# Causal masks of five batches moved from VectorE to GpSimd, and half a batch's loads reshaped, in an attention and mixer kernel

## The chip, the cores and the metric

The kernel runs on one core of one Trainium2 chip. A core has TensorE (matmul; the profile shows its matmuls as PE and its weight loads as PEld), VectorE (DVE), ScalarE (ACT), GpSimd (POOL) and SyncE (SP, which here only issues DMAs). The metric is the device time of one execution in microseconds (us), the median of several runs.

## The reference

Causal attention with a bias from a running sum, then a low rank mix along the sequence and a two layer feed forward block along the channels:

```python
B, H, S, D = 8, 8, 576, 64
scores = q @ k.T / sqrt(D)
cum = cumsum(max(s, 0), axis=-1)
scores = where(causal, -1e9, scores + minimum(-(cum[:, None] - cum[None, :]), 0))
attn = softmax(scores)                       # per batch and head
x = (attn @ v) as [B, S, H * D]              # 8 x 576 x 512
u = x + ((x.T @ U) @ V).T                    # U 576x32, V 32x576
out = u + maximum(u @ w_ch1, 0) @ w_ch2      # 512 -> 2048 -> 512
```

Inputs and output are float32; the kernel computes in bf16 with float32 accumulation.

## The kernel before

**Work units.** The 64 heads are taken in 32 pairs, n = 0 to 31, four pairs to a batch (`PB = 4`, so batch b has n = 4b to 4b + 3). Each pair passes through three generators, whose `yield`s are the points at which other work may be put between:

- `transposes(n)` (T): q and k of the pair, loaded with the sequence on 72 partitions, are turned by TensorE (L314) into PSUM and copied by VectorE or ACT into one of the `slot` tiles (L334 or L337). Rows of the running sum come into the same slot by a DMA on SP's queue (L298), so that the bias is part of the score matmul.
- `scores(n)` (S): score matmuls, transposed, keys on partitions (L401); ACT takes the exponential into a tile `pT` in four instructions, two of 128x1024 for the near blocks of the two heads (L416), one for the middle (L427), one of 128x128 for the tail (L433). The causal masks follow: the four diagonal blocks of each head (128x512) and the tail blocks of both heads (128x128), three masks for a pair.
- `values(n)` (V): matmuls of `pT` with v (L461); VectorE takes a reciprocal of the row sums (L470) and scales (L471) into `x_sb`. From batch 2 on, `x_sb` is also transposed by a DMA on SP (L478) into `xT`.

When a batch is done, `seqmix(b)` makes u transposed, `uT`, from it (VectorE: L499, L505, L515). The rows of u are then taken in nine groups of 512 by `chanmix(g)`: hidden layer matmuls (L647), ReLU on ACT (L807), then the second layer by seven products on quarters (L692) with sums on VectorE before (L674) and after (L706), and a store. `u_sd`, u with the sequence on partitions again, comes from a DMA transpose on SP (L814). In group 1 VectorE also makes sums of the weights (L256).

**Order.** TensorE and GpSimd run in program order (`in_program_order`). Up to n = 9 the order is a written list of steps (`weave`). From n = 8 a loop goes over n and does in each turn `transposes(n + 1)`, `scores(n)`, `values(n - 1)`; between their steps `step_fill` puts in steps of the waiting `chanmix`. At the first pair of a batch `load(b + 1)` comes ahead of that and `load_v(b + 1)` at the end; `seqmix(b - 1)` is spread over the second pair. For VectorE, ACT and SP the program order is fixed in the first part only; later a scheduler sets it, so an edit can move an instruction on SP's queue.

**Masks.** `mask(dst, n_tiles, w, on_pool=False)` (L342) either takes the minimum with a stored tile `keep` on VectorE (L346) or calls `causal` (L148), an `affine_select` on GpSimd (L149) that needs no second input. Batch 0 uses GpSimd through `masks(pT, True)`; for n = 4 to 31 `scores` calls `mask` without the last argument, so VectorE does it.

**Loads.** `load_qk(b, h, n)` (L108) issues the loads of q and k from GpSimd. Without runs (L116) a partition gets eight neighbouring tokens of a head (2 KB of source in one piece); the copies out of PSUM then write with a step, and take the tokens apart (L337). With runs (`in_runs`, b > 2, L111) partition p gets tokens p, p + 72, and so on, in pieces of 64 numbers; the copies then write with unit step (L334). `load(2)` is issued in two halves of four heads, later batches in one piece. `copies` (L288) picks ACT or VectorE. `pT` has two buffers, q and k have two each, slots rotate over three from n = 8 on, and v over two from batch 3 on.

Of the kernel before, what the change touches and what calls it, by code (L numbers as in the profile page):

```python
# [39 lines left out]
def kernel(  # L40
# [24 lines left out]
    PB = NP // B  # L65
# [12 lines left out]
    def pscore():  # L78
        return ps_s.tile([128, 1024], FP32, tag="s", name="pscore")

    def pwork():
        return ps_w.tile([128, 512], FP32, tag="w", name="pwork")
# [19 lines left out]
        q_t[b] = loads.tile([TP, H, TT * D], BF16, tag="q_sd", name="q_sd")  # L102
        k_t[b] = loads.tile([TP, H, TT * D], BF16, tag="k_sd", name="k_sd")

    def in_runs(b):
        return b > 2

    def load_qk(b, h, n):  # L108
        for dst, src in ((q_t[b], q), (k_t[b], k)):
            if in_runs(b):  # L110
                nc.gpsimd.dma_start(  # L111
                    out=dst[:, ds(h, n), :].rearrange("p h (t d) -> p (h t) d", t=TT),
                    in_=src[b, ds(h, n)].rearrange("h (t p) d -> p (h t) d", p=TP),
                )
            else:
                nc.gpsimd.dma_start(  # L116
                    out=dst[:, ds(h, n), :],
                    in_=src[b, ds(h, n)].rearrange("h (p t) d -> p h (t d)", p=TP),
                )
# [6 lines left out]

    alloc_qk(0)
    load_qk(0, 0, 2)
    identity = consts.tile([128, 128], BF16)
    make_identity(nc, identity)  # L130
    load_qk(0, 2, 2)
    load_qk(0, 4, 2)
    load_qk(0, 6, 2)

# [13 lines left out]
    def causal(out, n, w):  # L148
        nc.gpsimd.affine_select(  # L149
            out=out,  # L150
            in_=out,
            compare_op=ALU.is_ge,
            fill=0.0,
            base=0,
            pattern=[[0, n], [1, w]],
            channel_multiplier=-1,
        )
# [45 lines left out]
    def slot_of(n):  # L203
        return slots[n % NSLOT if n < 2 * PB else (n + 1) % 3]
# [8 lines left out]
    def spin(n, dst):  # L213
        for _ in range(n):
            nc.tensor.matmul(
                dst, lhsT=busy[:, 0:128], rhs=busy[:, 0 : dst.shape[1]], start=True, stop=True
            )
# [70 lines left out]
    def copies(n, hh, par):  # L288
        b = n // PB
        on_act = hh == (n == 4) and ((n in (0, 1, 4, 8, 9) or n > 8 and n % PB == 2) or n == 2 and par == 0)  # L290
        return nc.scalar.copy if on_act else nc.vector.tensor_copy

    def transposes(n):
        b, hp = divmod(n, PB)
        slot = slot_of(n)
        if b > 0:
            for r, n_r, c in ((0, 3, 1), (3, 1, 0)):
                nc.sync.dma_start(  # L298
                    out=slot[ds(D + r, n_r), :, ds(c * S, S)],
                    in_=rows_hbm[ds(r, n_r), ds(2 * n, 2)],  # L300
                )
        tps = {}

        def turn(hh, c):
            if c == 0:
                tile = pwork()
                if (n, hh) == (3, 0):
                    spin(2, tile)
                tps[hh] = tile.bitcast(BF16)[:, : 2 * 4 * TP].rearrange(
                    "p (c t m) -> p c t m", c=2, t=4  # L310
                )
            src = (q_t[b], k_t[b])[c]
            for t2 in range(4):
                nc.tensor.transpose(  # L314
                    tps[hh][:, c, t2, :],
                    src[:, 2 * hp + hh, ds(t2 * 128, 128)],
                    identity[:TP, :TP],
                )

        if b == 0:  # L320
            for hh in range(2):
                turn(hh, 0)
            yield
        for hh in range(2):
            if b > 0:
                turn(hh, 0)
            turn(hh, 1)
            tp = tps[hh]
            dst = slot[0:D, hh, 0 : 2 * S]
            for par in range(2):  # L330
                src = tp[par * D : par * D + D]
                if in_runs(b):
                    by_run = dst.rearrange("p (c t two m) -> p c t two m", c=2, t=4, two=2)
                    copies(n, hh, par)(by_run[:, :, :, par, :], src)  # L334
                else:
                    in_turn = dst.rearrange("p (c m t two) -> p c m t two", c=2, t=4, two=2)
                    copies(n, hh, par)(  # L337
                        in_turn[:, :, :, :, par], src.rearrange("p c t m -> p c m t")
                    )
            yield  # L340

    def mask(dst, n_tiles, w, on_pool=False):  # L342
        if on_pool:
            causal(dst, n_tiles, w)
        else:
            nc.vector.tensor_tensor(  # L346
                dst, dst, keep[:, :, 0:w].to_broadcast([128, n_tiles, w]), op=ALU.min
            )
# [48 lines left out]
    def scores(n, pT, spins=()):  # L397
        slot = slot_of(n)

        def mm(dst, hh, j, lo, hi):  # L400
            nc.tensor.matmul(  # L401
                dst,
                lhsT=slot[0:KA, hh, ds(S + j * 128, 128)],
                rhs=slot[0:KA, hh, lo:hi],
                start=True,
                stop=True,
            )

        tail = None
        for hh in range(2) if n > 0 else ():  # L410
            near = pscore()
            for j in range(4):
                mm(near[:, ds(j * 128, 128)], hh, j, j * 128, j * 128 + 128)
            mm(near[:, 512:960], hh, 0, 128, S)
            mm(near[:, 960:1024], hh, 3, 512, S)
            nc.scalar.activation(pT[:, hh, 0:1024], near, EXP, scale=scale)  # L416
            if n >= PB:
                mask(pT[:, hh, 0:512].rearrange("p (a b) -> p a b", a=4), 4, 128)
            if spins:
                tail = tail or pwork()  # L420
                spin(spins[hh], tail)
            yield
        mid, tail = pscore(), tail or pwork()
        for hh in range(2):
            mm(mid[:, ds(hh * 512, 320)], hh, 1, 256, S)
            mm(mid[:, ds(hh * 512 + 320, 192)], hh, 2, 384, S)
        nc.scalar.activation(  # L427
            pT[:, :, 1024:1536], mid.rearrange("p (a b) -> p a b", a=2), EXP, scale=scale
        )
        yield  # L430
        for hh in range(2):
            mm(tail[:, ds(hh * 64, 64)], hh, 4, 512, S)
        nc.scalar.activation(  # L433
            pT[:, :, 1536:1600],
            tail[:, 0:128].rearrange("p (a b) -> p a b", a=2),
            EXP,
            scale=scale,
        )
        if n >= PB:
            mask(pT[:, :, 1536:1600], 2, 64)  # L440
        yield


# [444 lines left out]

    act, dve = nc.scalar.copy, nc.vector.tensor_copy
    S0, S1, S2, S3 = (scores(n, pT_of(n), {1: (2, 3), 3: (2, 0)}.get(n, ())) for n in range(PB))  # L890
    T0, T1, T2, T3 = (transposes(n) for n in range(PB))
    M0, M1, M2, M3 = (mix_first(dt, act) for dt in range(PB))
    A, B_ = (near_by_rows(hh, pT_of(0)) for hh in range(2))
# [82 lines left out]
    def weave(order):  # L976
        for word in order.split():
            if word == "F":
                fill_with(1)
                continue  # L980
            kind, n = word[0], int(word[1:])
            if word not in made:
                if kind == "T":
                    made[word] = transposes(n)
                elif kind == "S":
                    made[word] = scores(n, pT_of(n))
                elif kind == "V":
                    made[word] = values(n, pT_of(n))
                else:
                    made[word] = seqmix(n)  # L990
            step(made[word])
            step_fill()
# [15 lines left out]
    for n in range(2 * PB, NP + 2):  # L1008
        b, hp = divmod(n, PB)
# [62 lines left out]
```

The softmax here doesn't subtract the row's maximum and nothing guards it: scores larger than these inputs give would overflow.

## Time and profile before

| What | Value |
|---|---|
| median of 10 runs (lowest, highest) | 367.28 us (367.01, 367.47) |
| profiled execution | 368.38 us |
| its span, first to last instruction | 366.6 us |
| busy PE, DVE, ACT, POOL | 353.3, 261.8, 204.5, 83.3 us |
| GpSimd's DMA queue q0 | 104,640 packets, 18.49 MB |
| SP's DMA queue q1 | 42,680 packets, 18.11 MB |
| a mask on DVE, 128x512 / on POOL, 128x512 (medians) | 416 ns / 650 ns |
| a copy L337 on DVE / L334 on DVE (medians) | 804 ns / 454 ns |
| granted TensorE clock | 1.00 |

Busy times are unions of an engine's instructions; a busy TensorE is not TensorE at its peak, since its ends are modelled. The chain of waits follows the last instruction back to what released it, step by step. A line number names the line of the kernel that made an instruction. Times inside the span count from its start. Waiting costs time only where the waiting engine is the one that sets the end.

### The profile page before, as it was taken

What the parts mean: (1) busy time and instruction counts of PE and PEld (TensorE: products, weight loads), DVE (VectorE), ACT (ScalarE), POOL (GpSimd) and SP (SyncE); (2) the same over time, 40 slices, a digit from 0 to 9 for tenths busy, and PEclk for the clock granted to TensorE, in tenths of its full rate; (3) what the DMA queues carried; (4) which work ended last, traced back from release to release, by engine and by line L of the source; (5) the groups of instructions that cost most, each with busy time, mean ns of one, the idle gap of its engine ahead of it and who ended that gap; (6) DMA issues with size and microseconds to landing.
All of it is one profiled execution on the core that took longest, in us unless ns stands there. A gap on an engine that the chain in (4) does not pass through costs nothing.

```text
span 366.6 us, 9382 instructions
## 1 busy us (share of the span) xinstructions
PE 353.3 (96%) x3915; PEld 248.5 (68%) x3959; DVE 261.8 (71%) x575; ACT 204.5 (56%) x309; POOL 83.3 (23%) x108
## 2 busy tenths in 40 slices
PE   8998999999999999999999999999999999999995
PEld 3675566665588667876689667876697568477484
DVE  8874776779798758995699559974897178075075
ACT  3873985756663578347843686357734630631720
POOL 8997434404030403140214022000000000000000
PEclk9999999999999999999999999999999999999999
DMA  7999999999949899979994999461014202403202
GB/s 102 175 197 203 169 196 109 158 148 99 105 39 96 145 134 70 100 87 132 128 98 63 143 134 84 58 157 21 18 48 118 64 18 84 91 5 109 61 29 88
DMA packets 147650, 37.40 MB, mean 102 GB/s; under 512 B 130648, under 2 KB 145976, under 8 KB 147608
## 3 DMA queue, kind: packets, MB, share of 16 engines
q0 software_dynamic: 104640, 18.49, 77.6%
q1 hardware_dynamic: 42680, 18.11, 26.4%
q8 instruction: 31, 0.51, 0.6%
q10 hardware_dynamic: 288, 0.20, 0.2%
q14 instruction: 11, 0.09, 0.1%
HBM read 37.25 MB, written 9.70 MB: 128 GB/s over the span
## 4 chain that ended last, share of the span: by engine, by line
PE 76%; DVE 14%; ACT 5%; issue 3%; DMA 1%; DVEq 0%; ACTq 0%
PE pwork L647 28%; PE pwork L692 21%; PE pscore L401 9%; PE pwork L461 7%; PE pwork L314 3%; PE pwork L657 3%; DVE slot L337 3%; ACT hT L807 2%; DVE uT L515 2%; DVE o_sb L706 2%; ACT pT L416 2%; DVE slot L674 2%; PE pscore L363 1%; PE pscore L647 1%; DVE pT L346 1%
## 5 line engine op out<-in xcount | busy, mean ns | idle before, releaser
L647 PE MATMUL pwork<-uT,w_sb 128*128 128x512 bf16 x525 | 133.6, 379 | 3.1 <-DVE x_sb L471 0.8
L807 ACT ACTIVATE hT<-pwork 128x512 bf16<-128x512 f32 x140 | 84.3, 606 | 62.3 <-PE pwork L647 62.2
L416 ACT ACTIVATE pT<-pscore 128x1024 bf16<-128x1024 f32 x56 | 57.2, 1030 | 55.0 <-PE pscore L401 54.1
L647 PEld LDWEIGHTS <-w_sb 128*128 128x128 bf16 x576 | 50.8, 98 | 50.9 <-issue 1.2
L401 PE MATMUL pscore<-slot 68*128 68x320 bf16 (+1 forms) x500 | 56.0, 246 | 0.2
L401 PEld LDWEIGHTS <-slot 68*128 68x128 bf16 x564 | 41.3, 97 | 16.7 <-issue 1.3
L692 PEld LDWEIGHTS <-hT 128*128 128x128 bf16 x496 | 46.2, 98 | 7.5 <-issue 0.7
L185 POOL DMA_DIRECT2D v_slot<-in_v_dram x36 | 30.3, 856 | 81.9 <-PE pwork L461 75.6
L692 PE MATMUL pwork<-w_sb,hT 128*128 128x256 bf16 x384 | 47.5, 273 | 0.0
L346 DVE TENSOR_TENSOR pT<-pT,keep 128x512 bf16<-128x512 bf16 (+1 forms) x81 | 28.6, 353 | 20.8 <-ACT pT L416 14.9
L461 PEld LDWEIGHTS <-pT 128*128 128x128 bf16 x870 | 32.4, 98 | 5.3 <-issue 0.6
L461 PE MATMUL pwork<-v_slot,pT 128*128 128x65 bf16 x870 | 35.5, 193 | 0.2 <-DVE uT L515 0.2
L334 DVE COPY slot<-pwork 64x576 bf16<-64x576 bf16 x70 | 31.6, 452 | 4.5 <-PE pwork L314 3.9
L692 PE MATMUL pwork<-w_sum,slot 128*128 128x256 bf16 x256 | 31.5, 272 | 0.8 <-DVE o_sb L706 0.7
L471 DVE TENSOR_TENSOR x_sb<-pwork,rec 128x320 bf16<-128x320 f32 x64 | 31.1, 488 | 1.3
L337 DVE COPY slot<-pwork 64x576 bf16<-64x576 bf16 x35 | 28.1, 802 | 5.5 <-PE pwork L314 3.5
L427 ACT ACTIVATE pT<-pscore 128x1024 bf16<-128x1024 f32 x29 | 30.2, 1042 | 2.6 <-PE pscore L401 2.4
L674 DVE TENSOR_TENSOR slot<-hT 128x1024 bf16<-128x1024 bf16 x16 | 11.0, 687 | 24.5 <-ACT hT L807 24.3
L470 DVE RECIPROCAL rec<-pwork 128x5 f32<-128x5 f32 x64 | 11.9, 189 | 22.9 <-PE pwork L461 22.7
L692 PEld LDWEIGHTS <-slot 128*128 128x128 bf16 x256 | 24.1, 98 | 4.5 <-issue 1.6
L706 DVE TENSOR_TENSOR o_sb<-o_sb,pwork 128x512 f32<-128x512 f32 (+2 forms) x34 | 21.9, 648 | 1.0 <-PE pwork L692 0.3
L111 POOL DMA_DIRECT2D q_sd<-in_q_dram x5 | 11.2, 2239 | 48.7 <-PE pwork L314 46.3
(128 smaller groups left out, 413.8 us busy)
## 6 DMA issues: line engine op xcount, KB each, us to landing
out_dram<-o_sb SPq DMA_DIRECT2D x35, 256.0 KB
w_sb<-in_moe_w_ch_dram POOLq DMA_DIRECT2D x4, 1024.0 KB, 12.7
v_slot<-in_v_dram POOLq DMA_DIRECT2D x28, 128.0 KB, 6.5
q_sd<-in_q_dram POOLq DMA_DIRECT2D x5, 576.0 KB, 12.1
k_sd<-in_k_dram POOLq DMA_DIRECT2D x5, 576.0 KB, 18.1
q_sd<-in_q_dram POOLq DMA_DIRECT2D x4, 288.0 KB, 12.5
k_sd<-in_k_dram POOLq DMA_DIRECT2D x4, 288.0 KB, 12.2
q_sd<-in_q_dram POOLq DMA_DIRECT2D x4, 144.0 KB, 4.9
```

The lines of the kernel that those rows point to most:

```text
L185: nc.gpsimd.dma_start(out=vt[:rows_t, t, :, 0:D], in_=v[b, :, ds(t * 128, rows_t), :].rearrange("h p d -> p h d"),)
L334: copies(n, hh, par)(by_run[:, :, :, par, :], src)
L337: copies(n, hh, par)(in_turn[:, :, :, :, par], src.rearrange("p c t m -> p c m t"))
L346: nc.vector.tensor_tensor(dst, dst, keep[:, :, 0:w].to_broadcast([128, n_tiles, w]), op=ALU.min)
L401: nc.tensor.matmul(dst, lhsT=slot[0:KA, hh, ds(S + j * 128, 128)], rhs=slot[0:KA, hh, lo:hi], start=True, stop=True,)
L416: nc.scalar.activation(pT[:, hh, 0:1024], near, EXP, scale=scale)
L427: nc.scalar.activation(pT[:, :, 1024:1536], mid.rearrange("p (a b) -> p a b", a=2), EXP, scale=scale)
L461: nc.tensor.matmul(po[:, i, :], lhsT=pT[:, hh, ds(place(j, i), 128)], rhs=vt[:, j, h, :], start=(j == 0), stop=(j == i), skip_group_check= ...
L471: nc.vector.tensor_tensor(x_sb[:, hp, :, ds(hh * D, D)], po[:, :, 0:D], rec.to_broadcast([128, 5, D]), op=ALU.mult,)
L647: nc.tensor.matmul(f1, lhsT=w1_sb[:, kt, ds(nf * 128, 128)], rhs=u[:, kt, :], start=(kt == 0), stop=(kt == 3),)
L692: nc.tensor.matmul(acc[:, i, :], lhsT=a[:, kt, ds(i * 128, 128)], rhs=b[:, kt, :], start=(i == 0 and kt == 0), stop=(kt == HF - 1), skip_g ...
L807: nc.scalar.activation(hT[:, nf, :], f1, RELU)
```

## The change

Two edits. The masks of n = 12 to 31 (batches 3 to 7) are made on GpSimd by `affine_select`; those of n = 4 to 11 stay on VectorE. And the second half (heads 4 to 7) of batch 2's q and k is loaded in runs, so that the copies of n = 10 and 11 have unit step. No other function changes.

```diff
-    def in_runs(b):
-        return b > 2
+    def in_runs(b, h):
+        return b > 2 or b == 2 and h >= 4
 
     def load_qk(b, h, n):
         for dst, src in ((q_t[b], q), (k_t[b], k)):
-            if in_runs(b):
+            if in_runs(b, h):
                 nc.gpsimd.dma_start(
...
                 src = tp[par * D : par * D + D]
-                if in_runs(b):
+                if in_runs(b, 2 * hp):
                     by_run = dst.rearrange("p (c t two m) -> p c t two m", c=2, t=4, two=2)
...
             if n >= PB:
-                mask(pT[:, hh, 0:512].rearrange("p (a b) -> p a b", a=4), 4, 128)
+                mask(pT[:, hh, 0:512].rearrange("p (a b) -> p a b", a=4), 4, 128, n >= 3 * PB)
...
         if n >= PB:
-            mask(pT[:, :, 1536:1600], 2, 64)
+            mask(pT[:, :, 1536:1600], 2, 64, n >= 3 * PB)
```

On GpSimd's queue, in program order, three `affine_select` now stand at each pair from n = 12 on, between the loads that were alone there. On SP's queue the scheduler puts the rows of n = 25 (one of their two DMAs) behind a u_sd transpose, two stores and an xT transpose instead of ahead of them. The orders of TensorE and ACT are the same, apart from the copies of n = 10 having the other form.

## The prediction

> **What bounds the kernel now.** I read the page's table of busy times first, then what TensorE waited for, then busy time by stage, and last the chain of waits inside two short stretches.
>
> ```profile
> PE 353.3 (96%) x3915; PEld 248.5 (68%) x3959; DVE 261.8 (71%) x575; ACT 204.5 (56%) x309; POOL 83.3 (23%) x108
> ```
>
> TensorE is the bound: it is idle for 13.3 us of 366.6. By stage (columns: window, its length, then busy PE, PEld, DVE, ACT, POOL with counts):
>
> ```profile
> 78.00:100.00 22.00, 20.91 (x249) 13.11 (x250) 18.51 (x40) 15.06 (x24) 4.45 (x2) 1.00 2.17 118
> 100.00:292.00 192.00, 189.15 (x2258) 139.73 (x2281) 146.82 (x347) 112.33 (x172) 30.30 (x26) 1.00 0.93 92
> 292.00:360.00 68.00, 67.66 (x503) 46.32 (x506) 38.17 (x64) 24.44 (x41) 0.00 (x0) 1.00 0.21 54
> ```
>
> The change acts from 36 us on and its masks from 102 to 282 us. There TensorE is idle 1.1 us (78 to 100) and 2.9 us (100 to 292), part of it records that the trace lacks. So no relief of another engine can bring more than about 4 us, plus what modelled ends hide. What TensorE waited for, over the whole span:
>
> ```profile
> PE pwork L647 <- DVE x_sb L471: 0.8, 2, 0.6
> PE pwork L692 <- DVE o_sb L706: 0.7, 2, 0.4
> PE pwork L647 <- ACT hT L807: 0.7, 2, 0.5
> PE pwork L461 <- DVE uT L515: 0.2, 1, 0.2
> ```
>
> The first, second and fourth row are VectorE being late. Where it is late, the chain of waits shows what stands in front. First near 86 us (batch 2's last copies, then masks), then near 188 us:
>
> ```profile
> 85.84 0.80 DVE slot L337
> 86.66 0.80 DVE slot L337
> 87.46 0.57 DVE w_sum L256
> 88.03 0.33 DVE pT L346
> ...
> 90.94 0.47 DVE x_sb L471
> ```
>
> ```profile
> 188.13 0.22 DVE pT L346
> 188.35 1.86 DVE uT L515 x4
> 190.21 0.61 DVE o_sb L706
> ```
>
> Both things that the change takes off VectorE (strided copies L337, masks L346) stand on a chain that stops TensorE, but each stop is only 0.2 to 0.6 us as shown. A 72 column matmul is shown with 195 ns although four of them take 0.29 us, so one issues each 32 ns or so, and a shown idle time hides about 0.16 us more.
>
> **What the skill says.** The Trainium skill, "GPSIMD Engine Reference", section on performance versus the Vector engine, says that GpSimd does elementwise work at about half of VectorE's speed. The trace agrees in direction: a mask of 128x512 takes 650 ns on POOL (L149) and 416 on DVE (L346), a factor of 1.6. "SBUF — State Buffer", section "Who interferes with whom", says that a VectorE instruction with two SBUF inputs contends with a GpSimd instruction that reads SBUF, one of the two blocking until the other ends, and that one with at most one SBUF input does not, outside of 2-port modes. Half is seen here: all VectorE copies L337 (PSUM input) lie within 783 to 819 ns, those beside POOL's batch 0 masks included. No L149 overlaps a two input DVE instruction before, so the blocking is not shown. "DMA: Bandwidth & Descriptors", section on why small descriptors are slow, says that short packets carry a fixed overhead each. The trace agrees: 36 to 58 us, with many kilobyte packets, moved 177 GB/s, 58 to 78 us, nearly all under 512 B, 133 GB/s.
>
> **Part 1, batch 2's second half in runs.** Pairs n = 10 and 11 have eight copies. Two (n = 10, first head) run on ACT, six on DVE. DVE: 6 x (804 - 454) ns = 2.1 us saved. ACT: 2 x (799 - 634) = 0.3 us saved. In the stretch from 80.1 to 91.4 us VectorE never rests, but not all 2.1 us come through: with the copies done near 85.4, the masks of n = 10 still wait for their exponentials, the last of which ends at 89.2 us in the timeline. From there: mask 0.22, L256 0.60, two reciprocals 0.26, L471 0.47, so L471 ends near 90.8 instead of 91.4 us. That is 0.6 us of a stop of 0.60 + 0.16. Small stops at 83.7 (0.16 shown, behind ACT) and 100.2 us (0.16, behind L471) may shrink too. I take 0.8 us gained, ends 0.4 and 1.3.
>
> Its costs: two loads of 288 KB go from L116 to L111. On POOL, L111 took 2.24 us for 576 KB, so about 1.1 us (my estimate, half) against 0.70, twice: +0.8 us at 42 to 44 us. Behind them in POOL's order stand memsets and five loads of v for batch 2, which already wait for older loads (idle 0.72, 2.79, 1.03 us before them), and no reader before 79.9 us (first values of n = 8), so nothing follows on TensorE. On the DMA engines 576 packets of 1 KB become 4608 of 128 B. From the 18,424 packets that the GpSimd queue moved in the 20 us of 58 to 78, 4608 take 5.0 us, against some 3.3 us for 590 KB at 177 GB/s: everything behind is 2 to 4 us later. The last of it, k of batch 3, issued at 59.0 and landed 18.1 us later, at 77; its first reader is the transposes of n = 12 at 90.4 us. Late by 4 us it still has 9 us. Batch 2's own second half lands near 58 to 62, its reader is at 78.5 us. Cost on the path: nothing, bounds 0 and 0.3.
>
> **Part 2, masks of n = 12 to 31.** Removed from DVE: 40 of 128x512 and 20 of 128x128, in the window answer 21.3 us between 102 and 292 us. Added on POOL: 40 x 0.65 + 20 x 0.30 = 32 us, on an engine busy 30 of 192 us there. The stops behind DVE in that window are 0.30 us at 190.9, 0.41 at 230.8 and 0.19 at 117.4, or 0.90 shown, 1.4 with hidden ends. Each stretch (110 to 118, 182 to 192, 222 to 232) holds 1.06 us of masks, more than its stop. The 0.49 us at 262.7 is behind ACT and stays. I take 0.8 us gained, ends 0 and 1.4, less than all since part of DVE's time is given back to contention.
>
> The new wait: values of n (L461) now wait for POOL. They start late: the last mask of n = 30 ends at 281.3 by the pT rows, its values are at 290.6 and those of n = 29, n = 30 at 274.4 and 281.0; the shortest distance from a mask's end to its values is 5.4 us (n = 30), most are 6.6 or 11. POOL runs a pair's masks in 1.5 us, the last some 0.1 us later than DVE: covered. Queued ahead of masks on POOL are L111 (4.5 us) and L185 (4.2 us). L185 waits for the old values (143.66, 180.61, 218.06 us) and ends at 147.9, 184.8, 222.3, about when the first exponentials of n = 17, 21, 25 end (147.7, 184.7, 222.0): at most 0.3 us.
>
> What moves: loads of q, k for batches 5, 6, 7 now stand behind the masks of n = 15, 19, 23. They were issued at 121.9, 158.7, 196.3 us as soon as transposes let go (POOL had waited 11 us); they will be issued near 135, 172, 209. The k load took 17.2 to 21.7 us, issued 2.2 us later: landed at about 155, 196, 233. First readers: transposes of n = 20, 24, 28 at 165.0, 202.5, 239.8 us. 6 us remain in the worst case. SP's queue shares the DMA engines: its u_sd transpose at 200.9 took 8.0 us behind the present load and will be freed of it, while slot rows and xT after 209 get more company; the rows of n = 25 are 0.6 us of issue later, 9 us before their scores at 220. Cost: nothing, bounds -0.3 and +1.
>
> **Sum.** 0.8 + 0.8 = 1.6 us. Against the profiled execution (368.38 us, span 366.6 and 1.8 around it) that is 366.8; the median of ten runs is 1.1 us below that execution, so 367.28 - 1.6 = 365.7.
>
> **Rivals.**
> (a) TensorE hides it all: the stops pass to ACT, which holds the third row of the waits, or to the next VectorE instruction. Then 0.1 to 0.7 us gained: 366.9. For it: every stop is short. Against: in these stretches ACT is far less busy than VectorE (15.1 against 18.5 of 22 us from 78 to 100).
> (b) **Slower: VectorE and GpSimd block each other.** Place: the ends of channel mixing, where L674 (0.68 us, two SBUF inputs) and L706 with u_sd follow one another while masks of n = 13, 17, 21, 25, 29 run. If each POOL mask holds VectorE for its whole length, a pair costs 2 x 0.65 + 0.30 = 1.6 us where 1.06 was saved: 0.54 us worse, and the same at the neighbours n = 12, 16, 18, 22, 26, 30. Eleven pairs x 0.54 = 5.9 us of VectorE, of which about half reaches TensorE, less 0.8 of part 1: +2.1, or 369.4. It decides once more than 65% of the mask time falls on VectorE. Against: in 182 to 190 us two input instructions fill 3.3 of 8 us, over the window some 38 of 190, and where VectorE starts first it is POOL that waits, which has 5 us.
> (c) Late loads: a landing stretched by a third makes transposes of n = 24 or 28 wait; 1 us each for two of them, 367.7 with the gain of the main case taken off.
>
> **Chances.** Main case 0.56 (own range 364.5 to 366.5), (a) 0.22, (b) 0.14, (c) 0.08. One measurement of this kernel can tell 0.2%, about 0.7 us, from no change. Faster by more: 0.58; within: 0.22; slower: 0.20. Range 364.4 to 368.5: the main case with both gains at their ends, (a), (c) and the mild part of (b).
>
> **What would show it.** Right: L337 falls from 48 to 40 instructions, L346 from 84 to 24, L149 reaches 73 (with keep); the waits of L647 on x_sb and of L692 on o_sb shrink; POOL near 115 us. Wrong: L674 or L706 longer than 0.69 us or idle in front of them behind POOL (rival b); L314 or L461 waiting for DMA or POOL (c); waits of TensorE on ACT grown by what those on DVE lost (a).

## The result: slower by 0.8%, and the profile after

| | changed kernel | before |
|---|---|---|
| median of its runs | 370.14 us (14 runs) | 367.36 us (48 runs) |
| ratio, 95% interval | 1.0083 (1.007 to 1.0096) | |
| profiled execution, span | 373.28, 371.2 us | 368.38, 366.6 us |

The forecast was 365.7. Some executions of any of these kernels run slower at a lower TensorE clock, and all medians here leave them out. The profiled execution of the changed kernel is not a typical one: TensorE was granted 0.83 of its clock in its first 30 us, and 1.00 in the stretches from 30 to 300 us. The same kernel was therefore run again (label after_again, 369.59 us median of 6, ratio 1.0063, 1.0051 to 1.0075), with clock 1.00 throughout and a span of 368.5 us, and details are read from that execution. The two series of the same kernel differ by 0.6 us, which is a measure of how far medians of so few runs can be trusted.

What was to change did change. First the busy times on the page of the changed kernel's first profile, then its groups of L337 and L346 on VectorE (busy us and mean ns of one, then idle time before them) and the answer on line L149 (durations are minimum, median, maximum in ns, both shapes together):

```profile
PE 357.3 (96%) x3915; PEld 250.4 (67%) x3959; DVE 247.0 (67%) x515; ACT 204.5 (55%) x309; POOL 121.6 (33%) x168
```

```profile
L337 DVE COPY slot<-pwork 64x576 bf16<-64x576 bf16 x29 | 23.2, 801 | 7.8 <-PE pwork L314 5.0 <-ACT slot L337 2.5
L346 DVE TENSOR_TENSOR pT<-pT,keep 128x512 bf16<-128x512 bf16 (+1 forms) x21 | 7.4, 350 | 5.5 <-ACT pT L416 3.3 <-ACT pT L433 2.1
```

```profile
L149 POOL TENSOR_SCALAR_AFFINE_SELECT pT<-pT x66: 292/634/1458, 15.8 to 285.4; 128x512 bf16<-128x512 bf16 x44, 128x128 bf16<-128x128 bf16 x22
```

VectorE issues 60 instructions less and is busy 14.8 us less. That is less than the 23 us of the instructions removed or shortened. In part other VectorE instructions became longer: in the second execution L674, and L706 where it reads u_sd, take 4.2 us more than before. The rest was not worked out; records of neighbouring instructions overlap, and the union counts an overlap once. TensorE, whose work is the same, lost the stops that the forecast named and got others. Its waits, in the second execution (engine and line, what released it, then us in total, times, longest):

```profile
PE pwork L461 <- DVE uT L515: 2.7, 4, 1.0
PE pscore L535 <- DVE ux L505: 1.4, 2, 0.7
...
PE pwork L692 <- DVE uT L515: 0.5, 1, 0.5
```

L692 behind o_sb (0.7 us before) and L647 behind ACT (0.7 before) are gone, and L647 behind x_sb has gone from 0.8 to 0.2. In their place stand 3.2 us behind L515, the addition of xT at the end of sequence mixing (0.2 before), and 1.4 us behind L505, a small copy in the same stage. What L515 and L505 were late for is not in these rows. For L515 the answer on the tile xT says it (us and times that L515 waited), and the chain of waits shows one case (start, length, what), with the record of L515 below it:

```profile
  DMA xT<-x_sb: 3.4, 3
```

```profile
142.93 0.40 DVE x_sb L471
143.33 0.03 DVE hT L674
143.36 8.99 DMA xT<-x_sb
152.35 0.02 issue
152.37 0.04 DVE uT L515
...
153.18 0.62 PE pwork L461 x15
```

```profile
152.37 1.09 DVE L515 TENSOR_TENSOR uT<-pwork,xT 128x320 bf16<-128x320 f32 x3 [1.32 <-DMA xT<-x_sb]
```

After the last values of a batch SP issues the DMA transpose of its last quarter. It was under way for 9.0 us, and VectorE stood idle for the last 1.3 us of it. For L505 the timeline of GpSimd and VectorE near 184 us says it (start, length, engine, line, operation; idle time before it in brackets):

```profile
184.19 0.75 POOL L149 TENSOR_SCALAR_AFFINE_SELECT pT<-pT 128x512 bf16<-128x512 bf16 x1
184.36 1.12 DVE L674 TENSOR_TENSOR hT<-hT 128x1024 bf16<-128x1024 bf16 x1
...
185.10 0.87 POOL L149 TENSOR_SCALAR_AFFINE_SELECT pT<-pT 128x512 bf16<-128x512 bf16 x1 [0.17 <-ACT pT L416]
185.40 1.11 DVE L674 TENSOR_TENSOR v_slot<-hT,slot 128x1024 bf16<-128x1024 bf16 x1
...
186.54 0.29 DVE L505 CAST ux<-pwork 128x128 bf16<-128x128 f32 x1
...
186.89 0.39 PE L535 MATMUL pscore<-V_sb,ux 32*128 32x512 bf16 x2 [0.67 <-DVE ux L505]
```

Two of the sums L674 take 1.12 and 1.11 us instead of 0.68 while a mask runs on GpSimd, so the copy L505 behind them comes some 0.9 us later, and TensorE waits for it.

### The profile page after: what moved, and what is told of

Its sections match the earlier page's. It is cut to its first block, busy times and chain, and to the rows that moved or that the text cites. A ratio compares the mean times of both kernels' runs of the same rounds, so it can differ in the third digit from the quotient of the medians.

```text
span 371.2 us, 9388 instructions
## 1 busy us (share of the span) xinstructions
PE 357.3 (96%) x3915; PEld 250.4 (67%) x3959; DVE 247.0 (67%) x515; ACT 204.5 (55%) x309; POOL 121.6 (33%) x168
## 4 chain that ended last, share of the span: by engine, by line
PE 78%; DVE 7%; DMA 7%; issue 3%; ACT 3%; POOL 1%; DVEq 0%; ACTq 0%; POOLq 0%
PE pwork L647 29%; PE pwork L692 20%; PE pscore L401 9%; PE pwork L461 7%; DMA xT<-x_sb 5%; PE pwork L314 4%; PE pwork L657 3%; DVE slot L674 2%; DMA q_sd<-in_q_dram 2%; DVE o_sb L706 1%; DVE uT L515 1%; ACT hT L807 1%; PE pscore L647 1%; DVE slot L337 1%; PE pscore L363 1%
## 5 line engine op out<-in xcount | busy, mean ns | idle before, releaser
L647 PE MATMUL pwork<-uT,w_sb 128*128 128x512 bf16 x525 | 133.7, 379 | 1.8 <-DVE x_sb L471 0.2
L647 PEld LDWEIGHTS <-w_sb 128*128 128x128 bf16 x576 | 50.5, 98 | 49.4 <-DVE x_sb L471 0.5
L149 POOL TENSOR_SCALAR_AFFINE_SELECT pT<-pT 128x512 bf16<-128x512 bf16 (+1 forms) x66 | 39.4, 600 | 127.5 <-ACT pT L416 105.3
L401 PE MATMUL pscore<-slot 68*128 68x320 bf16 (+1 forms) x500 | 57.3, 250 | 0.4 <-ACT pT L427 0.2
L401 PEld LDWEIGHTS <-slot 68*128 68x128 bf16 x564 | 42.1, 99 | 17.7 <-issue 2.5
L692 PEld LDWEIGHTS <-hT 128*128 128x128 bf16 x496 | 46.1, 98 | 7.5 <-issue 0.7
L692 PE MATMUL pwork<-w_sb,hT 128*128 128x256 bf16 x384 | 47.5, 273 | 0.0
L334 DVE COPY slot<-pwork 64x576 bf16<-64x576 bf16 x76 | 34.4, 452 | 4.9 <-PE pwork L314 4.0
L461 PEld LDWEIGHTS <-pT 128*128 128x128 bf16 x870 | 32.4, 97 | 7.0 <-issue 2.3
L461 PE MATMUL pwork<-v_slot,pT 128*128 128x65 bf16 x870 | 35.5, 194 | 1.6 <-DVE uT L515 1.6
L692 PE MATMUL pwork<-w_sum,slot 128*128 128x256 bf16 x256 | 31.5, 273 | 0.5 <-DVE uT L515 0.4
L674 DVE TENSOR_TENSOR slot<-hT 128x1024 bf16<-128x1024 bf16 x16 | 11.3, 706 | 28.4 <-ACT hT L807 28.4
L337 DVE COPY slot<-pwork 64x576 bf16<-64x576 bf16 x29 | 23.2, 801 | 7.8 <-PE pwork L314 5.0
L692 PEld LDWEIGHTS <-slot 128*128 128x128 bf16 x256 | 24.0, 98 | 4.1 <-issue 1.2
L706 DVE TENSOR_TENSOR o_sb<-o_sb,pwork 128x512 f32<-128x512 f32 (+2 forms) x34 | 21.9, 648 | 2.3 <-PE pwork L692 1.4
L314 PEld LDWEIGHTS <-q_sd 72*128 72x128 bf16 x256 | 15.2, 100 | 9.9 <-DMA q_sd<-in_q_dram 1.6
```

The source lines that it names most:

```text
L149: nc.gpsimd.affine_select(out=out, in_=out, compare_op=ALU.is_ge, fill=0.0, base=0, pattern=[[0, n], [1, w]], channel_multiplier=-1,)
L314: nc.tensor.transpose(tps[hh][:, c, t2, :], src[:, 2 * hp + hh, ds(t2 * 128, 128)], identity[:TP, :TP],)
L401: nc.tensor.matmul(dst, lhsT=slot[0:KA, hh, ds(S + j * 128, 128)], rhs=slot[0:KA, hh, lo:hi], start=True, stop=True,)
L461: nc.tensor.matmul(po[:, i, :], lhsT=pT[:, hh, ds(place(j, i), 128)], rhs=vt[:, j, h, :], start=(j == 0), stop=(j == i), skip_group_check= ...
L647: nc.tensor.matmul(f1, lhsT=w1_sb[:, kt, ds(nf * 128, 128)], rhs=u[:, kt, :], start=(kt == 0), stop=(kt == 3),)
L692: nc.tensor.matmul(acc[:, i, :], lhsT=a[:, kt, ds(i * 128, 128)], rhs=b[:, kt, :], start=(i == 0 and kt == 0), stop=(kt == HF - 1), skip_g ...
```

## Experiments

**Theory A**, formed from these rows, has three terms: part 1 gains about what was forecast; the loads of q and k that now stand behind masks on GpSimd's queue run into the xT transposes (the larger loss); and masks on GpSimd hold up VectorE's two-input sums (the smaller loss). The rivals: all of the loss is the holding up (B), it is TensorE's clock (C), or part 1 has no gain (D). All runs below are timed beside the kernel before on the same chip; it took 367.32, 367.38 and 367.32 us in the three groups.

### The same kernel again

> The changed kernel once more, for a second profile. Theory A (two causes: late xT transposes behind the moved loads, and VectorE held up by GpSimd's masks): about 2.5 to 3 us slower than before, four stops of TensorE of 0.7 to 1.0 us again, at the seqmix of n = 17 and 25 (VectorE L515 waiting for a DMA into xT) and of n = 21 and 29 (L505 late, L674 longer than 0.69 us in front of it). Rival C (the half speed clock of 10 us at the start of the first profile is the change's doing): it is there again.

Measured: 369.59 us. The waits above repeat, the low clock at the start does not: not C.

### Part 1 alone

```diff
-                mask(..., 4, 128, n >= 3 * PB)
+                mask(..., 4, 128)
```

(and likewise for the 128x128 mask, here and in later runs where only the 128x512 form is shown)

> Part 1 alone: half of batch 2's loads in runs, all masks from n = 4 on VectorE. Theory A: 1.0 us faster than before (ratio 0.997), since the first profile of the change was 1.1 us ahead between the transposes of n = 10 and n = 13, after its start is taken off; L515 never waits for xT. Rival D (the longer packet trains of this part cost later): same or slower than before.

Measured: 366.32 us (5 runs), ratio 0.997 (0.9958 to 0.9982). So part 1 gains 1.0 us, and no wait of L515 for xT shows. TensorE's longest waits after its start:

```profile
PE pwork L692 <- DVE o_sb L706: 0.7, 2, 0.4
PE pwork L647 <- ACT hT L807: 0.5, 1, 0.5
```

The stops of L647 behind x_sb have fallen from 0.8 to 0.2, those behind L706 are as before, those behind ACT are 0.2 shorter. D falls.

### Late loads, nearly no masks

Part 1, with only the 128x128 mask of n = 15, 19 and 23 on GpSimd. These three small instructions wait for the last exponentials of their pair, and the loads of batches 5, 6, 7 stand behind them.

```diff
-            mask(pT[:, :, 1536:1600], 2, 64)
+            mask(pT[:, :, 1536:1600], 2, 64, n in (15, 19, 23))
```

> Part 1, and of part 2 just one 128x128 mask each of n = 15, 19 and 23 on GpSimd, so that the loads of batches 5 to 7 stand behind it, at about 137, 175 and 213 us, with hardly any mask work on GpSimd. Theory A: L515 waits 0.8 to 1.2 us for xT near n = 17 and n = 25, L674 stays at 0.69 us; 1.5 to 1.9 us slower than part 1 alone. Rival B (port blocking alone costs the time): as part 1 alone, within 0.3 us.

Measured: 368.52 us (14 runs), ratio 1.0045 (1.0024 to 1.0066), 2.2 us above part 1 alone, more than the 1.5 to 1.9 expected. No L674 is above 0.693 us, so none of these sums is held up; the waits of L515 for xT are there (on the tile xT, us and times):

```profile
  DMA xT<-x_sb: 2.3, 3
```

Three instructions of 0.3 us on an engine that rests most of the time cost 2.2 us, by what is queued behind them. B falls.

### Early loads, all masks on GpSimd

The changed kernel, with the loads of batches 5, 6, 7 put two pairs earlier in the program, ahead of the masks of n = 14, 18, 22.

```diff
-        if hp == 0 and b < B - 1:
+        if n == 2 * PB or n == 3 * PB:
             load(b + 1)
...
+        if hp == 2 and b > 2 and b + 2 < B:
+            load(b + 2)
```

> The changed kernel with the loads of batches 5 to 7 issued ahead of the masks of n = 14, 18, 22, that is where they were before. Theory A: no wait of L515 for xT, 1.5 to 1.9 us faster than the changed kernel; the stops at n = 21 and 29 with long L674 stay. Rival B: as the changed kernel, within 0.3 us.

Measured: 367.02 us (22 runs), ratio 0.9996 (0.9981 to 1.001): 2.6 us faster than the changed kernel, again more than expected. No L515 waits for xT, while L674 still reaches 1.12 us and the two stops at L535 remain. What moved is the issue of the loads, here the first one of batch 5 in the second execution of the changed kernel and with early loads (start, length; idle time before it in brackets):

```profile
133.00 2.24 POOL L111 DMA_DIRECT2D q_sd<-in_q_dram  x1
```

```profile
119.94 2.24 POOL L111 DMA_DIRECT2D q_sd<-in_q_dram  x1 [8.05 <-PE pwork L314]
```

The cause of the late transpose can be seen in the DMA's busy share from 138 to 153 us in 40 slices (a digit is tenths, a slice 0.375 us). First the changed kernel again, then early loads:

```profile
DMA  9999999999999999999999999999999999999999
```

```profile
DMA  9963000000000059998999999999999987100000
```

The xT transpose is issued at 143.36 and 143.47 us. With early loads the DMA engines have just been idle for 4 us; in the changed kernel they are in the middle of q, k (k issued at 135.24 instead of 122.17) and then of v. The Trainium skill, page "Trainium Kernel Development and Optimization", section "Key Constraints", says that DMAs issued from SP's and GpSimd's queues run on the same 16 DMA engines and interleave; this is what is seen, with 9.0 us for a transpose that with early loads was in by 151.1 us (7.6 us at most), when L515 read it without waiting:

```profile
151.08 1.08 DVE L515 TENSOR_TENSOR uT<-pwork,xT 128x320 bf16<-128x320 f32 x3
```

SP's queue is not the cause there: around 143 us it holds the same transfers in the same order in both kernels and in the one before. A busy share of 9 is not by itself the sign of a late transpose: the next one of this kind, at 179.78 us with early loads, was also issued at a share of 9, and nothing waited for it. What differs both times is how much is queued: GpSimd's queue moved 15,168 packets from 138 to 153 us in the changed kernel, 14,497 in late loads and 4,907 with early loads, and from 176 to 192 us 15,171 in the changed kernel against 7,102 with early loads. Whether the packets of q and k or those of v are the ones in the way was not separated.

### Part 2 alone

```diff
-        return b > 2 or b == 2 and h >= 4
+        return b > 2
```

> Part 2 alone: the masks of n = 12 to 31 on GpSimd, batch 2 loaded as before. Theory A: part 1's gain of 1.1 us is missing from the changed kernel and all of its loss is here: 370.5 (370.2 to 371), with waits of L515 for xT and L674 above 1.1 us. Rival G (moved loads and masks lose less without the 128 byte packets of batch 2, the parts don't add): 369.6 or less.

Measured: 370.70 us (5 runs), ratio 1.0087 (1.0071 to 1.0104): 1.1 us above the changed kernel's second series and 0.6 above its first. Within that, the parts add, and G falls.

### Early loads, masks that only write

The early loads kernel, each mask of n = 12 to 31 replaced by a memset of the same elements. The causal masking of these pairs is left out.

```diff
-        if on_pool:
+        if on_pool and not isinstance(on_pool, str):
             causal(dst, n_tiles, w)
+        elif on_pool:
+            nc.gpsimd.memset(dst, 1.0)
...
-                mask(..., 4, 128, n >= 3 * PB)
+                mask(..., 4, 128, "memset" if n >= 3 * PB else False)
```

> The early loads kernel, with each GpSimd mask of n = 12 to 31 replaced by a GpSimd memset (1.0) of the same elements: GpSimd writes what the mask wrote, at the same place in its queue, and reads nothing; the causal masking of these pairs is left out. Theory A (the two block each other through GpSimd's reads of SBUF): every L674 at 0.70 us or less, the stops at L535 behind L505 gone, 366.0 to 366.5. Rival F (any access of GpSimd to SBUF, or its lateness in some other way, holds L674 up): L674 again near 1.1 us beside the memsets of n = 21 and 29, and the time near 367.0 (somewhat less if a memset is shorter than a mask).

Measured: 366.42 us (19 runs), ratio 0.9987 (0.9966 to 1.0008). This median does not separate it from early loads; the trace does. On VectorE's line of the sums (here L676, as the kernel has two lines more; minimum, median, maximum in ns), first early loads, then this kernel:

```profile
L674 DVE TENSOR_TENSOR hT<-hT x16: 678/684/1120, 98.2 to 350.4; 128x1024 bf16<-128x1024 bf16 x16
```

```profile
L676 DVE TENSOR_TENSOR hT<-hT x16: 680/684/686, 97.6 to 348.7; 128x1024 bf16<-128x1024 bf16 x16
```

One of these sums ran from 183.12 to 183.81 us, in its usual 0.69 us, with a memset from 183.25 to 183.78 beside it. The two stops at L535 are gone, and the span of the profiled execution is 363.4 us against 365.2, both at clock 1.00. So GpSimd's writes alone do not hold VectorE up, and F falls. What the mask does beyond them is to read, though it is also another instruction than the memset. That the reads are the cause is what the Trainium skill, page "SBUF — State Buffer", section "Who interferes with whom", says: a VectorE instruction with two SBUF inputs contends with a GpSimd instruction that reads SBUF, not with one that only writes. The lengths agree roughly with one waiting for the other's end: in the second execution of the changed kernel the mask that began at 184.19 ended at 184.94, and the sum begun at 184.36 took 0.54 us more from there, against 0.68 us for a whole one. The 1.8 us in span do not all belong to the reads: a memset is shorter than a mask (0.53 against 0.63 us), and 0.7 us are a wait of TensorE for rows of a slot (L401), which the second profile of early loads below does not have.

### How much is the holding up worth?

Three runs put some masks back on VectorE, with loads early. First those of n = 13, 17, 21, 25, 29:

```diff
-                mask(..., 4, 128, n >= 3 * PB)
+                mask(..., 4, 128, n >= 3 * PB and n % PB != 1)
```

> The early loads kernel, with the masks of n = 13, 17, 21, 25, 29 (the pairs whose masks stand beside the end of channel mixing) back on VectorE. Theory A (GpSimd's masks hold up VectorE's two-input L674 there, and this is what is left of the loss): no L674 above 0.70 us, TensorE's waits at L535 behind L505 (1.4 us in two stops) gone, 0.7 us less than the early loads: 366.3, about as part 1 alone. Rival E (what is left of the loss is other masks, or the reads of GpSimd slow VectorE a little everywhere): L674 short again, but the time stays near 367.0.

Measured: 366.56 us (7 runs), ratio 0.9994 (0.9963 to 1.0025), inconclusive. The stops at L535 are gone as expected, but L674 still takes 1.12 and 1.11 us beside the masks of n = 12 and 16: the choice of pairs was too narrow. There it stops nobody.

Then those of both pairs of each four that touch L674, part 1 and early loads again on the same chip:

```diff
-                mask(..., 4, 128, n >= 3 * PB)
+                mask(..., 4, 128, n >= 3 * PB and n % PB > 1)
```

> The early loads kernel with the masks of both pairs of each four that stand beside L674 (n = 12, 13, 16, 17, 20, 21 and so on) back on VectorE; those of n = 14, 15, 18, 19, 22, 23, 26, 27, 30, 31 stay on GpSimd. Theory A: no L674 above 0.72 us, no stop at L535 behind L505, and the time falls from the early loads' 367.0 to part 1's 366.3, within 0.3. Rival E (half of the masks on GpSimd still costs something elsewhere): 366.8 or more. If VectorE's relief counted for anything it would be 366.0 or less.

> Part 1 alone once more, on the same chip as the two others, to be compared with them: 366.3, within 0.3.

> The early loads kernel once more, on the same chip: theory A 367.0, that is 0.7 above part 1 alone, with L674 at 1.1 us beside n = 21 and 28 and the two stops at L535. If it comes within 0.3 of part 1, the cost of blocking isn't shown.

Measured: 366.72 us (14 runs, ratio 0.9979, 0.9958 to 1.0), 366.56 (9 runs, 0.9989, 0.9967 to 1.0011) and 367.06 (13 runs, 0.9995, 0.9979 to 1.001). In the first, no L674 is above 0.693 us. Early loads stand 0.5 us above part 1 alone, outside the 0.3 that was set as the bound, and 0.7 in the first group. So with the loads early the masks on GpSimd bring nothing and probably cost 0.5 to 0.7 us; the intervals of this group overlap. How much of it is the holding up is not shown: early half, without the masks beside L674, is 0.3 us below early loads and 0.2 above part 1, both too small to be told from nothing, and it misses the 366.3 expected, so rival E (its masks still cost something elsewhere) is not decided either. The waits say why it is so little. Early loads again, then early half:

```profile
PE pscore L535 <- DVE ux L505: 1.4, 2, 0.7
```

```profile
PE pwork L692 <- DVE o_sb L706: 0.8, 2, 0.5
...
PE pwork L647 <- ACT hT L807: 0.6, 1, 0.6
```

Either kernel has 1.4 us of such stops. (The profile of early half also has two waits for DMA of 0.7 us each, at L401 and L314, which are left out here.) With the masks of those pairs on GpSimd the old stops vanish and new ones come at L535; with them on VectorE it is the other way about.

### Only the masks of n = 17 and 25 on GpSimd

Part 1, and the masks of two pairs that stand beside the end of channel mixing but in the changed kernel lengthened L674 little (to 0.94 us at most). The next loads of q and k behind them come three pairs later.

```diff
-                mask(..., 4, 128)
+                mask(..., 4, 128, n in (17, 25))
```

> Part 1, and only the masks of n = 17 and 25 on GpSimd: no load stands behind them (loads are issued ahead of them), and in the changed kernel L674 was not long beside these two. What is left of stops behind VectorE at L692 near 188 us is 0.4 us. Theory A: as part 1 alone or 0.1 to 0.3 us faster, 366.0 to 366.4, with L674 at 0.70 or less. Rival H (masks on GpSimd cost wherever L674 or L706 are near): L674 above 1 us beside n = 17 or 25, 366.7 or more.

Measured: 366.13 us (7 runs), ratio 0.9962 (0.9947 to 0.9977). L674 reaches 0.777 us once, L692 behind o_sb falls from 0.7 to 0.3 us, and 0.3 us appear behind L515. H falls. It is faster than the kernel before and the changed kernel, and the best here of those that make all masks, but not to be told from part 1 alone (366.32).

## Why the prediction was wrong

Forecast: 0.8 + 0.8 us gained. Measured, as differences of medians in the first group: part 1 −1.0 (367.32 to 366.32); late loads +2.2 (to 368.52); the remaining masks on GpSimd +1.1 (to 369.59). The sum is +2.3 us.

- **Part 1 was right.** Six copies less at L337, the stop of L647 behind x_sb from 0.8 to 0.2 us, and 1.0 us gained against 0.8, within its ends 0.4 and 1.3. Its extra packets are 5,376 on the page of GpSimd's queue, not the 4,032 of the forecast (4,608 less 576), and cost nothing that the traces show.
- **The failed step is "What moves".** It saw that the loads of batches 5 to 7 would be issued later and said when: near 135, 172, 209 us. In the second execution they went at 133.00, 171.01 and 209.54. It then asked who reads these loads, found 6 us to spare, and wrote: cost nothing, bounds −0.3 and +1. The loads' own readers did wait little (L314 behind q_sd 0.7 us). Those who lost share nothing but the DMA engines with them: the xT transposes from SP's queue at 143 us, and again in the next two batches (L515 waited 1.3, 1.0 and 1.1 us). The step even said that xT would "get more company", though only after 209 us, and gave it no deadline. The last quarter of xT is read by L515 7.6 us after it is issued (early loads), and under way behind the moved loads it took 9.0. Measured cost: 2.2 us (late loads), 2.6 (changed kernel less early loads), against an upper bound of 1.
- **Rival (b) was half right**: its mechanism, given 0.14, is real. L674 went from 0.684 to 1.12 us where a mask reads beside it, in batch after batch. L706 with u_sd reached 1.01 us too. Its price was too high: it put half of 5.9 us on TensorE, and measured are 0.5 to 0.7 above part 1 with early loads, or 1.1 with late loads. It counted masks of eleven pairs, while in the second execution only four pairs (n = 12, 16, 21, 29) lengthen an L674 by more than 0.3 us, and of these only two (n = 21, 29) stop TensorE. That its 369.4 us lies close to what was measured is luck: most of the loss is that of the late loads.
- **Part 2's gain was there and was given back.** The o_sb stops that it aimed at did vanish (0.7 us as shown in part 1 alone), and so did the ACT stop (0.5) that it expected to stay. But 1.4 us came at L535. The forecast allowed for contention by taking 0.8 of 1.4 us; with early loads none of the 0.8 is left.
- **Rival (c)** named late loads and the wrong victim: transposes of n = 24 or 28. **Rival (a)**, stops passing to ACT, did not happen: L647 behind hT went.
- The new wait of values for masks on GpSimd cost nothing, as said: no L461 waits for POOL, neither its matmuls nor its weight loads, which read `pT`. POOL was busy 121.6 us against 115 forecast; masks that wait for VectorE count as busy (up to 1.46 us for one).

One reading of before could have pointed to the first case. Its chain and its waits could not, since they list only what was late. But the busy share of DMA from 138 to 153 us shows a pause, from about 141.4 to 145 us, at the end of which the xT transpose was issued (145.43 us):

```profile
DMA  9999999970001000000499999999999999999720
```

Loads moved 13 us later fill this pause, and each transfer that starts in the 20 us after their issue had to be listed with its reader's time. Before the xT transposes of the next two batches (182.00 and 219.82 us) there are only dips of about 1 us, so it is the list that matters more than the pause.

What stays open: the worth of the holding up by itself, between 0 and 0.7 us, which transfers ahead of xT make it late, and whether an xT with more spare time (issued earlier, or with its last quarter added later) would let the changed order stand; neither was tried.

## To carry to other kernels

When instructions are put on a queue that also issues DMAs, find the loads that come to stand behind them and then look not only at the readers of these loads but at every transfer that uses the DMA engines while they run: the one with the least spare time pays. Moving work from VectorE to GpSimd can lengthen VectorE's instructions with two SBUF inputs: look at each overlap, and above all at those that stand ahead of TensorE. Here there were two of these, and their price was small. And split a change of two parts before judging it: here one part alone is 0.3% faster, and the whole is 0.8% slower.

## What the runs showed of the hardware

- A sum of 128x1024 with both inputs in SBUF took 0.68 us alone, 0.69 beside a GpSimd memset and up to 1.12 beside a GpSimd mask; masks grew too, to as much as 1.46 us from 0.63 (beside two L706 with u_sd).
- A DMA transpose of the same tile was under way 9.0 us where 15,168 packets of GpSimd's queue passed from 138 to 153 us, and 7.6 us at most where 4,907 did. Nothing of it is in the record of its issue (1.23 us both times).
